# Random-feature projections of a pair's two heads: from one full-array product per slot to three products on each half of TensorE's rows

## The chip, the cores and the metric

The kernel runs on one core of one Trainium2 chip. What counts is the device time of one execution in microseconds (us), so lower is better. TensorE (PE in the profile) multiplies matrices: a weight load (PEld) puts the stationary operand in the array, and a matmul streams the moving operand past it into PSUM. VectorE (DVE), ScalarE (ACT) and GpSimd (POOL) do the elementwise work, SyncE (SP) issues the DMAs.

## What is computed

```python
B, H, S, D, M = 8, 8, 576, 64, 128           # batch, heads, tokens, head size, features
def phi(x):                                  # x already scaled by D ** -0.25
    h = einsum('bhsd,md->bhsm', x, omega) - sum(x * x, -1) / 2
    return exp(h - max(h, -1)) / sqrt(M)
q_p, k_p = phi(q_s), phi(k_s)
kv, z = k_p^T v, sum of k_p over tokens      # per head
attn = (q_p kv) / (q_p z + 1e-6)
x = attn as [4608 tokens, 512]
out = elu(x @ w_in) @ w_out                  # w_in 512 x 2048, w_out 2048 x 512, both float64
```

All in float32 precision. Attention is linear in the number of tokens; the two layers after it (the MLP) are most of the arithmetic.

## The kernel before

**Attention.** The 64 heads are taken as 32 pairs (two heads that lie side by side, `pair`). A pair's 1152 rows (2 x 576 tokens) make nine slots of 128 tokens: slot j < 8 belongs to head j % 2, and slot 8 holds the last 64 tokens of both heads. Each pair has a key side and a query side. `project` turns one side into the features `h` (128 tokens x 9 slots x 128 features); `kv` multiplies the key features with the values; `finish` spreads z over the partitions, divides the query features by their denominators, transposes them (`pt`) and multiplies them with kv (`pn`) into the MLP's input, split in a head `xh` and a tail `xl`.

**Two kinds of sides.** On a "native" side (`i < NNAT[nm]`: the first 7 key sides and 8 query sides) the projection is plain float32: the rows of x and their squares, 128 partitions deep, against `of` (omega over -SCALE/2). The profile counts two weight loads and two matmuls for each such float32 product. On the other 49 sides, x is split in a head `hi` (rounded to float32r) and a tail `lo` = x - hi, and omega in `oh` and `ol`. Before the change, hi and lo of one head lie above each other in the 128 rows (`t`, written by four copies and subtractions of 64 partitions), and one float32r matmul with 256 moving columns `[oh | ol]` (line 488) gives hi.oh + lo.oh in the left half and hi.ol + lo.ol in the right half of a PSUM bank. So there are nine such matmuls per side, two to a bank, five banks. ACT moves the right half and half the sum of squares to `p2` (line 497), DVE subtracts it from the left half and takes the largest value in the same operation (line 506), ACT negates it (line 410) and takes the exponential of `h` in SBUF (line 404).

**MLP.** Twelve blocks of 384 tokens and sixteen slices of 128 hidden features; the first three blocks go through in two halves of eight slices. One of the 192 steps is twelve matmuls of 384 columns (layer 1, three products of heads and tails for each of four chunks, lines 764 to 766, into `ph`), an ELU on ACT, DVE and POOL, and nine matmuls of 512 columns (layer 2, lines 798 to 800, into `acc`). Weights come as float64 and are converted by ACT, DVE and POOL during the first block.

**What sets the order.** Nothing is issued as the code reads. Every piece of work is a task (`op`) with an engine, an assumed time and a due time; `Plan.order` plays them through with these assumed times, giving each free engine the ready task with the earliest due time (some tasks may go to one of two engines), and the instructions are written in that order. Due times come from the constants at the head (`SEG`, `STEP`, `DUE_K`, `K2` and so on), the assumed time of a float32r matmul from `mm`. PSUM has eight banks: three `acc`, two `ph`, three `pa`; projections of later pairs, `pt` and `pn` share the three `pa`.

Of the kernel before, what the change touches and what calls it, by code (L numbers as in the profile page):

```python
# [14 lines left out]
ALU = mybir.AluOpType  # L15
# [25 lines left out]
NNAT = dict(k=7, q=8)  # L41
# [3 lines left out]
SEG = [8.62, 6.25, 4.29, 5.37, 3.5, 5.81]  # L45
STEP = 4.91
STEP_ATT = 6.59

LAG = 3.5


PAIR0 = 9.46
DUE_LOAD, DUE_K, DUE_KV, DUE_Q = 27.64, 24.71, 14.12, 18.02
LOAD2, K2, KV2, Q2 = 56.0, 46.17, 30.64, 29.89
TAIL = 11.71
TAIL2 = 4.06


CONV1 = 13.71
CONV_STEP = -0.51  # L60
CONV2 = 0.84
CONV3 = 70.47
# [5 lines left out]
DUE_Z = 12.0  # L68
# [195 lines left out]
def mm(n, m=1):  # L264

    return m * (n / 2.4 + 2.5)
# [15 lines left out]
def performer_elu_kernel(  # L282
# [31 lines left out]
    nc.vector.memset(of[D:P], -0.5 * SCALE)  # L314

# [22 lines left out]
    def omega(due):  # L338
        op("SP", 500, due + 0.005, lambda: nc.sync.dma_start(of[0:D], omT), (), ("of",), D * M * 4)
        t = Buf(sb, [P, M], F32, "junk", "omf", 2)  # L340
        due += 15
        for a in range(2):
            r = slice(a * D, a * D + D)
            op("SP", 500, due, lambda r=r: nc.sync.dma_start(t()[r], omT), (), ((t, a),), D * M * 4)
        op("DVE", dve(M), due + 3, lambda: nc.vector.tensor_copy(om[:, 0:M], t()), ((t, 0), (t, 1)), ("oh",))
# [22 lines left out]
    def bank(i, early, name):  # L368

        tag = early if i < NEARLY else "pa"  # L370
        return Buf(ps, [P, 512], F32, tag, name, dict(pa=3, ph=2).get(tag, 1))

# [21 lines left out]
    def project(i, nm, due):  # L394
# [6 lines left out]
        def exps(g, js, src, due, reads):  # L401
            def f():
                for j in js:
                    nc.scalar.activation(  # L404
                        h()[:, j, :], src(j), AF.Exp, bias=nb()[:, j:j + 1], scale=SCALE
                    )
            op("ACT", len(js) * act(M, native(i, nm), True), due, f, (*reads, (nb, g)), ((h, g),))

        def negate(g, js, due):
            op("ACT", act(4), due, lambda: nc.scalar.mul(nb()[:, js], mx()[:, js], -SCALE), ((mx, g),), ((nb, g),))  # L410

        if native(i, nm):
# [11 lines left out]
            for g in range(3):  # L424
                d = due + 2.2 * g
                p = bank(i, "acc%d" % g, f"pp{nm}_{i}_{g}")
                n = 4 if g < 2 else 1
                js = slice(4 * g, 4 * g + n)

                def mms(g=g, p=p):  # L430
                    for c in range(4 if g < 2 else 2):
                        t, a = 2 * g + c // 2, c % 2
                        if g < 2:
                            o = p()[:, c * M:(c + 1) * M]
                        else:
                            o = p()[a * D:a * D + D, 0:M]
                        nc.tensor.matmul(o, x()[:, a, t * P:min(t * P + P, S)], of, start=True, stop=True)

                def view(p=p):
                    return p().rearrange("p (j x) -> p j x", j=4)  # L440

                op("PE", 872 if g < 2 else 240, d, mms, [*((x, a, 2) for a in range(2)), "of"], (p,))
                op(
                    "DVE", 66 + n * 133, d + 1,
                    lambda js=js, n=n, view=view: nc.vector.tensor_reduce(mx()[:, js], view()[:, 0:n], AX.X, ALU.max),
                    (p,), ((mx, g),),
                )
                negate(g, js, d + 1.1)
                exps(g, range(js.start, js.stop), lambda j, g=g, view=view: view()[:, j - 4 * g], d + 1.5, (p,))
            return  # L450

        def t():
# [4 lines left out]
            lambda: nc.scalar.activation(t(), t(), AF.Square, scale=(SCALE * 0.5) ** 0.5), ((x, 3),), ((x, 3),),  # L457
# [3 lines left out]

        y = Buf(sb, [P, 2 * S], F32R, "t", f"t{nm}_{i}", 2)
        for a in range(2):
            r, o = slice(a * D, a * D + D), slice(D - a * D, P - a * D)
            cs = slice(a * S, a * S + S)
            parts = ((x, 0),)
            op(
                "ACT", act(S), due - 5 + a, lambda e, r=r, cs=cs: copy(e, y()[r, cs], x()[r, 0]), parts, ((y, a, "h"),),  # L470
                alt=other("y_hi", "DVE", dve(S, True)),
            )
            op(
                "POOL", pool(S), due - 4 + a,
                lambda e, r=r, o=o, cs=cs: tt(e, y()[o, cs], x()[r, 0], y()[r, cs].bitcast(F32), ALU.subtract),
                (*parts, (y, a, "h")), ((y, a, "l"),), alt=other("y_lo", "DVE", dve(S)),
            )
        for c in range(5):
            d = due + 1.1 * c
            p = Buf(ps, [P, 512], F32, "pa", f"pp{nm}_{i}_{c}", 3)  # L480
            p2 = Buf(sb, [P, 2, M], F32, "p2", f"p2{nm}_{i}_{c}", 2)
            n = 2 if c < 4 else 1
            g = 0 if c < 2 else 1

            def mms(c=c, p=p, n=n):
                for a in range(n):
                    o = a * (S + D) + c * P
                    nc.tensor.matmul(p()[:, a * 256:(a + 1) * 256], y()[:, o:o + P], om, start=True, stop=True)  # L488

            def view(p=p):  # L490
                return p().rearrange("p (a x) -> p a x", a=2)

            op("PE", mm(256, n), d, mms, [(y, a, z) for a in range(2) for z in "hl"] + ["oh", "om"], (p,))
            def rest(c=c, n=n, p2=p2, view=view):
                for a in range(n):
                    j = 2 * c + a
                    nc.scalar.activation(  # L497
                        p2()[:, a], view()[:, a, M:], AF.Identity, bias=sq()[:, j:j + 1], scale=-1.0
                    )

            op("ACT", n * act(M, True, True), d + 0.5, rest, (p, sq), (p2,))

            def ttr(c=c, n=n, p2=p2, view=view):
                for a in range(n):
                    j = 2 * c + a
                    nc.vector.tensor_tensor_reduce(  # L506
                        out=h()[:, j, :], in0=view()[:, a, 0:M], in1=p2()[:, a, :], scale=1.0, scalar=LOWEST,
                        op0=ALU.subtract, op1=ALU.max, accum_out=mx()[:, j:j + 1],
                    )

            op("DVE", n * 212, d + 1, ttr, (p, p2), ((h, g, c), (mx, g)))
            if c in (1, 4):
                js = range(0, 4) if c == 1 else range(4, NJ)
                negate(g, slice(js.start, js.stop), d + 1.1)
                exps(g, js, lambda j: h()[:, j, :], d + 1.5, [(h, g, e) for e in range(5)])

    def parts_of(i, nm):
        h = st[i]["h" + nm]
        return [(h, g) for g in range(3 if native(i, nm) else 2)]
# [38 lines left out]
    def finish(i, due):  # L558
# [15 lines left out]
        for g in range(3):  # L574
            d = due - 9 + g
            js = slice(4 * g, min(4 * g + 4, NJ))
            n = js.stop - js.start
            slots = [(j, j % 2, slice(0, P)) for j in range(4 * g, 4 * g + 4)]
            if g == 2:
                slots = [(8, a, slice(a * D, a * D + D)) for a in range(2)]  # L580
            hg = (h, g) if native(i, "q") else (h, min(g, 1))

            def dens(slots=slots):
                for j, a, r in slots:
                    junk = Buf(sb, [P, M], F32, "junk", f"junk_{i}_{j}_{a}", 2)
                    nc.vector.tensor_tensor_reduce(  # L586
                        out=junk()[r], in0=h()[r, j, :], in1=pz()[r, a * P:(a + 1) * P], scale=1.0, scalar=EPS,
                        op0=ALU.mult, op1=ALU.add, accum_out=den()[r, j:j + 1],
                    )

            def dg(js=js):
                return den()[:, js]

            op("DVE", len(slots) * 210, d, dens, (hg, pz), ((den, g),))
# [4 lines left out]
                    e, h()[:, js], h()[:, js], den()[:, js].unsqueeze(2).to_broadcast([P, n, M]), ALU.mult  # L599
# [5 lines left out]
            def turn(g=g, p=p, js=js):  # L605
                for e, j in enumerate(range(js.start, js.stop)):
                    nc.tensor.transpose(p()[:, e * P:(e + 1) * P], h()[:, j, :], ident)  # L607

            def src(g=g, p=p):
                if g == 2:  # L610
                    return p()[:, 0:P].rearrange("p (a x) -> p a x", a=2)
                return p().rearrange("p (t a x) -> p a t x", t=2, a=2)

            def dst(x, g=g):
                if g == 2:
                    return x[:, :, 512:S]
                return x[:, :, g * 256:(g + 1) * 256].rearrange("p a (t x) -> p a t x", t=2)
# [332 lines left out]
```

## Time and profile before

| | |
|---|---|
| device time, three runs | median 1089.97 us (1088.09 to 1090.83) |
| profiled execution, span from first to last instruction | 1090.7 us, the only time given for it |
| PE busy | 1060.6 us, 97% of the span, 5971 matmuls |
| PE weight loads busy | 936.8 us (86%) |
| ACT, DVE, POOL busy | 724.7 us (66%), 635.9 us (58%), 404.4 us (37%) |
| DMA | 176.90 MB, 162 GB/s |

In the rows of the timeline a matmul's own time includes its way through the array, so the times of two that follow each other overlap; what one costs is the distance from its start to the start of the next. A row with xN is N instructions in a row, merged. `128*128` is the number of active rows and columns of the array; `128*64` uses half of the columns, and two such matmuls can stand beside each other.

### The profile page before, as it was taken

The numbers are of one execution on the slowest core, as the hardware profiler recorded it, in microseconds if no ns is written. First come the engines' busy times: TensorE is split into PE (matmuls) and PEld (weight loads), VectorE is DVE, ScalarE is ACT, GpSimd is POOL, SyncE is SP. The second block draws the span as 40 slices with busy tenths as digits, with TensorE's granted clock in tenths as the row PEclk, the third lists the DMA queues.
The fourth block names the chain that finished last, engine by engine and source line by source line (L and its number), as shares of the span: only waits on it lengthen the run. The fifth ranks groups of instructions, "written<-read, shape, count | busy, mean of one in ns | idle before, by whom it ended". The sixth has DMA issues, their size and how long they took to land.

```text
span 1090.7 us, 19072 instructions
## 1 busy us (share of the span) xinstructions
PE 1060.6 (97%) x5971; PEld 936.8 (86%) x5971; DVE 635.9 (58%) x2403; ACT 724.7 (66%) x2027; POOL 404.4 (37%) x372
## 2 busy tenths in 40 slices
PE   7979888999999999999999999999999999999998
PEld 7867777889988888999888888899888888899987
DVE  6788988775776775225676666324566775322221
ACT  6878774546988986337888988326888888432222
POOL 3568746661223343222343233322233342222221
PEclk8889998999999999999999999999999999999999
DMA  7554656656663554434554645434444452343431
GB/s 213 171 181 161 208 188 240 218 186 205 207 205 130 169 170 150 165 118 157 176 155 153 193 139 170 162 119 150 162 155 167 157 164 79 117 164 119 161 121 63
DMA packets 53235, 176.90 MB, mean 162 GB/s; under 512 B 6032, under 2 KB 6224, under 8 KB 53136
## 3 DMA queue, kind: packets, MB, share of 16 engines
q1 hardware_dynamic: 53136, 175.69, 48.4%
q8 instruction: 48, 0.79, 0.3%
q14 instruction: 51, 0.42, 0.1%
HBM read 155.48 MB, written 20.19 MB: 161 GB/s over the span
## 4 chain that ended last, share of the span: by engine, by line
PE 79%; DVE 9%; ACT 6%; issue 3%; DMA 1%; POOL 1%; SPq 0%; DVEq 0%; POOLq 0%; ACTq 0%
PE ph L764 11%; PE acc L798 10%; PE acc L800 10%; PE ph L766 10%; PE acc L799 10%; PE ph L765 10%; PE pkv L535 4%; PE ppq L488 3%; PE pn L634 3%; PE pt L607 2%; PE ppk L488 2%; ACT hk L404 1%; DVE u_w L697 1%; DVE u_w L704 1%; DVE u_w L709 1%
## 5 line engine op out<-in xcount | busy, mean ns | idle before, releaser
L336 POOL TENSOR_TENSOR g<-e,g 128x384 fp32r<-128x384 f32 x182 | 189.2, 1040 | 547.7 <-DVE g L333 405.9
L764 PE MATMUL ph<-xh,w1c 128*128 128x384 f32 x768 | 267.5, 348 | 6.7 <-DVE e L777 6.2
L766 PE MATMUL ph<-xh,w1c 128*128 128x384 f32 x768 | 259.8, 338 | 0.0
L765 PE MATMUL ph<-xl,w1c 128*128 128x384 f32 x768 | 259.7, 338 | 0.0
L777 DVE SCALAR_TENSOR_TENSOR e<-e,ph 128x384 f32<-128x384 f32 x192 | 105.9, 552 | 237.2 <-ACT e L774 232.8
L798 PE MATMUL acc<-w2h,g 128*128 128x512 f32 x576 | 231.4, 402 | 0.0
L773 ACT ACTIVATE e<-ph 128x384 f32<-128x384 f32 x192 | 93.6, 488 | 206.4 <-PE ph L766 198.4
L800 PE MATMUL acc<-w2h,g 128*128 128x512 f32 x576 | 227.7, 395 | 0.0
L799 PE MATMUL acc<-w2l,g 128*128 128x512 f32 x576 | 227.4, 395 | 0.0
L764 PEld LDWEIGHTS ph<-xh,w1c 128*128 128x128 f32 x768 | 145.6, 190 | 20.1 <-DVE e L777 8.5
L765 PEld LDWEIGHTS ph<-xl,w1c 128*128 128x128 f32 x768 | 145.8, 190 | 7.2
L766 PEld LDWEIGHTS ph<-xh,w1c 128*128 128x128 f32 x768 | 145.4, 189 | 0.3 <-POOL w1c L336 0.3
L800 PEld LDWEIGHTS acc<-w2h,g 128*128 128x128 f32 x576 | 108.5, 188 | 25.5
L798 PEld LDWEIGHTS acc<-w2h,g 128*128 128x128 f32 x576 | 108.7, 189 | 15.1 <-issue 2.3
L799 PEld LDWEIGHTS acc<-w2l,g 128*128 128x128 f32 x576 | 108.8, 189 | 12.2
L336 POOL TENSOR_TENSOR hq<-hq,den 128x512 f32<-128x512 f32 (+1 forms) x96 | 90.4, 961 | 36.1 <-DVE den L595 24.6
L774 ACT ACTIVATE e<-e 128x384 f32<-128x384 f32 x192 | 100.7, 525 | 3.1
L333 DVE CAST g<-e 128x384 fp32r<-128x384 f32 x166 | 72.8, 439 | 23.5 <-PE acc L800 18.8
L586 DVE CUSTOM_DVE_ANT_0 junk<-hq,pz 128x128 f32<-128x128 f32 (+1 forms) x320 | 74.1, 279 | 16.9 <-PE pz L570 16.1
L506 DVE CUSTOM_DVE_ANT_0 hq<-ppq,p2q 128x128 f32<-128x128 f32 x216 | 54.3, 287 | 41.8 <-ACT p2q L497 40.2
L506 DVE CUSTOM_DVE_ANT_0 hk<-ppk,p2k 128x128 f32<-128x128 f32 x225 | 56.5, 286 | 36.1 <-ACT p2k L497 34.3
L497 ACT ACTIVATE p2q<-ppq,sqq 128x128 f32<-128x128 f32 x216 | 67.8, 367 | 12.5 <-PE ppq L488 10.8
(82 smaller groups left out, 1620.3 us busy)
## 6 DMA issues: line engine op xcount, KB each, us to landing
w1c<-w1s SPq DMA_DIRECT2D x176, 512.0 KB, 3.3
raw_w<-in_w_dram SPq DMA_DIRECT2D x32, 512.0 KB, 3.6
xk<-in_kx_dram SPq DMA_DIRECT2D x25, 576.0 KB, 3.9
xq<-in_qx_dram SPq DMA_DIRECT2D x24, 576.0 KB, 4.6
v<-in_v_dram SPq DMA_DIRECT2D x32, 325.0 KB, 3.4
out_dram<-o SPq DMA_DIRECT2D x36, 256.0 KB, 2.9
w1s<-w1c SPq DMA_DIRECT2D x16, 512.0 KB, 3.2
xq<-in_q_dram SPq DMA_DIRECT2D x8, 288.0 KB, 4.0
```

What stands on the lines that cost most here:

```text
L336: (nc.vector if e == "DVE" else nc.gpsimd).tensor_tensor(*args)
L506: nc.vector.tensor_tensor_reduce(out=h()[:, j, :], in0=view()[:, a, 0:M], in1=p2()[:, a, :], scale=1.0, scalar=LOWEST, op0=ALU.subtract, o ...
L586: nc.vector.tensor_tensor_reduce(out=junk()[r], in0=h()[r, j, :], in1=pz()[r, a * P:(a + 1) * P], scale=1.0, scalar=EPS, op0=ALU.mult, op1 ...
L764: nc.tensor.matmul(ph(), wh, xh[:, c, o:o + TB], start=(c == 0), stop=False)
L765: nc.tensor.matmul(ph(), wh, xl[:, c, o:o + TB], start=False, stop=False)
L766: nc.tensor.matmul(ph(), wl, xh[:, c, o:o + TB], start=False, stop=(c == NC - 1))
L773: op("ACT", act(TB, True), due, lambda: nc.scalar.activation(e(), ph(), AF.Relu, scale=-1.0), (p,), (e,))
L774: op("ACT", act(TB), due + 0.2, lambda: nc.scalar.activation(e(), e(), AF.Exp, scale=-1.0), (e,), (e,))
L777: lambda: nc.vector.scalar_tensor_tensor(e(), e(), -1.0, ph(), ALU.add, ALU.max), (p, e), (e,),
L798: nc.tensor.matmul(a(), g()[:, 0, ts], w2h[:, f], start=(f == f0), stop=False)
L799: nc.tensor.matmul(a(), g()[:, 0, ts], w2l[:, f], start=False, stop=False)
L800: nc.tensor.matmul(a(), g()[:, 1, ts], w2h[:, f], start=False, stop=(f == f1 - 1))
```

## The change

It replaces the projection of all sides that are not native and makes twelve sides native (5 key sides, 7 query sides) where there were fifteen.

- `t` now holds hi and lo in two planes of 128 rows: head 0 in rows 0 to 63, head 1 in rows 64 to 127. One copy and one subtraction of 128 partitions make it.
- Slots 0 to 7: for each of four chunks, three products hi.oh, lo.oh and hi.ol of 64 rows and 128 columns are summed in PSUM for either head (line 507), head 0 into one bank and head 1 into another, the two heads taking turns: 24 matmuls in one task.
- Slot 8: two float32 matmuls of 128 rows into 64 columns each (line 515), straight from x, against `oz`, which is omega in one half of its rows and zero in the other.
- `p2` is gone. DVE takes the largest values of four slots at once from PSUM (line 428), two small operations make the bias from it and the sum of squares (lines 482 and 483), and ACT takes the exponential from PSUM (line 419). Slots of one head now form a group, so groups take every second slot.
- The assumed time of a float32r matmul goes from n / 2.4 + 2.5 to n / 2.25 + 2.5 ns, and most due times are other ones.

```diff
-NNAT = dict(k=7, q=8)
+NNAT = dict(k=5, q=7)
-SEG = [8.62, 6.25, 4.29, 5.37, 3.5, 5.81]
-STEP = 4.91
-STEP_ATT = 6.59
+SEG = [10.92, 6.51, 5.27, 5.54, 3.5, 5.81]
+STEP = 5.77
+STEP_ATT = 5.1
...
+    oz = const.tile([P, 2, M], F32, name="oz")
+    nc.vector.memset(oz, 0.0)
...
-        y = Buf(sb, [P, 2 * S], F32R, "t", f"t{nm}_{i}", 2)
-        for a in range(2):
-            r, o = slice(a * D, a * D + D), slice(D - a * D, P - a * D)
...
-        for c in range(5):
...
-            def mms(c=c, p=p, n=n):
-                for a in range(n):
-                    o = a * (S + D) + c * P
-                    nc.tensor.matmul(p()[:, a * 256:(a + 1) * 256], y()[:, o:o + P], om, start=True, stop=True)
...
+        def bias(g, js, due):
+            def f():
+                r = cols(js)
+                nc.vector.scalar_tensor_tensor(mx()[:, r], mx()[:, r], SCALE, sq()[:, r], ALU.mult, ALU.subtract)
+                nc.vector.scalar_tensor_tensor(nb()[:, r], mx()[:, r], -1.0, sq()[:, r], ALU.mult, ALU.subtract)
...
+        y = Buf(sb, [P, 2, S], F32R, "t", f"t{nm}_{i}", 2)
...
+        banks = [bank(i, "acc%d" % g, f"pp{nm}_{i}_{g}") for g in range(3)]
+        terms = ((0, 0), (1, 0), (0, M))
+
+        def mms():
+            for c in range(4):
+                for n, (z, m) in enumerate(terms):
+                    for a in range(2):
+                        r, o = slice(a * D, a * D + D), a * D + c * P
+                        nc.tensor.matmul(
+                            banks[a]()[:, c * M:(c + 1) * M], y()[r, z, o:o + P], om[r, m:m + M],
+                            start=(n == 0), stop=(n == 2),
+                        )
+
+        def last():
+            for a in range(2):
+                o = (1 - a) * (S - D)
+                nc.tensor.matmul(
+                    banks[2]()[a * D:a * D + D, 0:M], x()[:, 0, o:o + D], oz[:, a], start=True, stop=True
+                )
+
+        op("PE", mm(M, 12), due, mms, ((y, "h"), (y, "l"), "oh", "om"), banks[0:2])
+        op("PE", 230, due + 2, last, ((x, 0), ("oz", 0), ("oz", 1)), banks[2:3])
```

On PE, here is the key side of pair 26, in the middle of the MLP's ninth block, before. `ppk` is the side's PSUM bank, `tk` its heads and tails, `ph` and `acc` are the MLP's.

```order
L765 MATMUL ph_132_9251<-xl_82,w1c_132_9031 128x384
L766 MATMUL ph_132_9251<-xh_81,w1c_132_9031 128x384
L488 MATMUL ppk_26_0_9280<-om_73,tk_26_9042 128x256 x2
L798 MATMUL acc_8_0_0_9108<-w2h_77,g_130_9152 128x512
L799 MATMUL acc_8_0_0_9108<-w2l_78,g_130_9152 128x512
L800 MATMUL acc_8_0_0_9108<-w2h_77,g_130_9152 128x512
L488 MATMUL ppk_26_1_9293<-om_73,tk_26_9042 128x256 x2
```

And the same side after; between the second and the third row stand the other 22 matmuls of line 507, `ppk_26_0` and `ppk_26_1` by turns.

```order
L507 MATMUL ppk_26_0_9215<-om_73,tk_26_9016 128x128
L507 MATMUL ppk_26_1_9217<-om_73,tk_26_9016 128x128
...
L813 MATMUL acc_8_0_0_9241<-w2h_79,g_128_8987 128x512
L814 MATMUL acc_8_0_0_9241<-w2l_80,g_128_8987 128x512
L815 MATMUL acc_8_0_0_9241<-w2h_79,g_128_8987 128x512
L779 MATMUL ph_132_9201<-xh_83,w1c_132_8996 128x384
L780 MATMUL ph_132_9201<-xl_84,w1c_132_8996 128x384
L781 MATMUL ph_132_9201<-xh_83,w1c_132_8996 128x384
L515 MATMUL ppk_26_2_9251<-oz_75,xk_26_8949 64x128 x2
L813 MATMUL acc_8_0_1_9259<-w2h_79,g_128_8987 128x512
```

Five short pieces spread between the MLP's matmuls have become one block of 24 and one of two, each with full-array matmuls on both sides. In the whole program, the places where PE goes over to products of half the array (64 rows or 64 columns) and back were 46; now they are 144.

On ACT, the same side before, from its first operation after the projection to its last:

```order
L497 ACTIVATE p2k_26_0_9300<-ppk_26_0_9280,sqk_26_8839 128x128 x2
L404 ACTIVATE hq_25_9182<-hq_25_9182,nbq_25_9233 128x128 x5
L774 ACTIVATE e_132_9290<-e_132_9290 128x384
L497 ACTIVATE p2k_26_1_9331<-ppk_26_1_9293,sqk_26_8839 128x128 x2
L497 ACTIVATE p2k_26_2_9338<-ppk_26_2_9317,sqk_26_8839 128x128 x2
L410 ACTIVATE nbk_26_9348<-mxk_26_9314 128x4
L497 ACTIVATE p2k_26_3_9350<-ppk_26_3_9325,sqk_26_8839 128x128 x2
L404 ACTIVATE hk_26_9313<-hk_26_9313,nbk_26_9348 128x128 x4
L497 ACTIVATE p2k_26_4_9375<-ppk_26_4_9353,sqk_26_8839 128x128
```

and after:

```order
L788 ACTIVATE e_132_9263<-ph_132_9201 128x384
L419 ACTIVATE hk_26_9268<-ppk_26_0_9215,nbk_26_9255 128x128 x4
L789 ACTIVATE e_132_9263<-e_132_9263 128x384
L419 ACTIVATE hk_26_9268<-ppk_26_1_9217,nbk_26_9255 128x128 x4
L419 ACTIVATE hk_26_9268<-ppk_26_2_9251,nbk_26_9255 128x128
L336 CAST tk_27_9339<-xk_27_9273 128x576
```

The nine operations of line 497 and the two of line 410 are gone, and the copy that makes `tk` of the next pair is one of 128 partitions where there were two of 64.

More of the change, by code (lines that the diff above doesn't have):

```diff
@@ L38 @@
 F64_MAX = float.fromhex("0x1.dffffep-96")
-NNAT = dict(k=7, q=8)
+NNAT = dict(k=5, q=7)
 MLP0 = 58
-SEG = [8.62, 6.25, 4.29, 5.37, 3.5, 5.81]
-STEP = 4.91
-STEP_ATT = 6.59
[L49 to L59, printed above, removed]
+SEG = [10.92, 6.51, 5.27, 5.54, 3.5, 5.81]
+STEP = 5.77
+STEP_ATT = 5.1
+LAG = 3.75
+PAIR0 = 8.73
+DUE_LOAD, DUE_K, DUE_KV, DUE_Q = 30.22, 22.83, 16.48, 18.02
+LOAD2, K2, KV2, Q2 = 56.0, 37.39, 30.64, 29.89
+TAIL = 14.11
+TAIL2 = 4.77
+CONV1 = 13.86
 CONV_STEP = -0.51
-CONV2 = 0.84
-CONV3 = 70.47
+CONV2 = 1.42
+CONV3 = 55.14
+PACE = 2.25
 SPLIT = (0, 8, 16)
 NHALF = 3
-DUE_Z = 12.0
+DUE_Z = 11.71
 NEARLY = 4
@@ L264, in mm @@
 def mm(n, m=1):
-    return m * (n / 2.4 + 2.5)
+    return m * (n / PACE + 2.5)
 def act(n, psum=False, ptr=False):
@@ L371, in bank, with slots, cols @@
         return Buf(ps, [P, 512], F32, tag, name, dict(pa=3, ph=2).get(tag, 1))
+    def slots(i, nm, g):
+        if g == 2:
+            return range(8, 9)
+        return range(4 * g, 4 * g + 4) if native(i, nm) else range(g, 8, 2)
+    def cols(js):
+        return slice(js.start, js.stop, js.step)
     def load_pair(i, due):
@@ L399, in project, with exps, largest @@
         mx, nb = small("mx" + nm, NJ, f"mx{nm}_{i}"), small("nb" + nm, NJ, f"nb{nm}_{i}")
-        def exps(g, js, src, due, reads):
+        def exps(g, js, p, due):
             def f():
-                for j in js:
+                for e, j in enumerate(js):
                     nc.scalar.activation(
-                        h()[:, j, :], src(j), AF.Exp, bias=nb()[:, j:j + 1], scale=SCALE
+                        h()[:, j, :], p()[:, e * M:(e + 1) * M], AF.Exp, bias=nb()[:, j:j + 1], scale=SCALE
                     )
-            op("ACT", len(js) * act(M, native(i, nm), True), due, f, (*reads, (nb, g)), ((h, g),))
-        def negate(g, js, due):
-            op("ACT", act(4), due, lambda: nc.scalar.mul(nb()[:, js], mx()[:, js], -SCALE), ((mx, g),), ((nb, g),))
+            op("ACT", len(js) * act(M, True, True), due, f, (p, (nb, g)), ((h, g),))
+        def largest(g, js, p, due):
+            n = len(js)
+            op(
+                "DVE", 66 + n * 133, due,
+                lambda: nc.vector.tensor_reduce(
+                    mx()[:, cols(js)], p()[:, 0:n * M].rearrange("p (j x) -> p j x", x=M), AX.X, ALU.max
+                ),
+                (p,), ((mx, g),),
+            )
         if native(i, nm):
@@ L437, in mms @@
                         nc.tensor.matmul(o, x()[:, a, t * P:min(t * P + P, S)], of, start=True, stop=True)
-                def view(p=p):
-                    return p().rearrange("p (j x) -> p j x", j=4)
                 op("PE", 872 if g < 2 else 240, d, mms, [*((x, a, 2) for a in range(2)), "of"], (p,))
+                largest(g, js, p, d + 1)
                 op(
-                    "DVE", 66 + n * 133, d + 1,
-                    lambda js=js, n=n, view=view: nc.vector.tensor_reduce(mx()[:, js], view()[:, 0:n], AX.X, ALU.max),
-                    (p,), ((mx, g),),
-                )
-                negate(g, js, d + 1.1)
-                exps(g, range(js.start, js.stop), lambda j, g=g, view=view: view()[:, j - 4 * g], d + 1.5, (p,))
+                    "ACT", act(4), d + 1.1,
+                    lambda js=js: nc.scalar.mul(nb()[:, cols(js)], mx()[:, cols(js)], -SCALE), ((mx, g),), ((nb, g),),
+                )
+                exps(g, js, p, d + 1.5)
             return
@@ L460, in project @@
         op("DVE", dve(S), due - 3, lambda: nc.vector.tensor_reduce(sq(), t(), AX.X, ALU.add), ((x, 3),), (sq,))
-        y = Buf(sb, [P, 2 * S], F32R, "t", f"t{nm}_{i}", 2)
-        for a in range(2):
-            r, o = slice(a * D, a * D + D), slice(D - a * D, P - a * D)
[L467 to L477, printed above, removed]
@@ L478, in project @@
-        for c in range(5):
[L479 to L483, printed above, removed]
-            def mms(c=c, p=p, n=n):
-                for a in range(n):
-                    o = a * (S + D) + c * P
[L488 to L515, printed above, removed]
@@ new lines, in bias @@
+        def bias(g, js, due):
[3 more added lines that the diff above has]
+                nc.vector.scalar_tensor_tensor(nb()[:, r], mx()[:, r], -1.0, sq()[:, r], ALU.mult, ALU.subtract)
+            op("DVE", 2 * dve(4), due, f, ((mx, g), sq), ((mx, g), (nb, g)))
+        y = Buf(sb, [P, 2, S], F32R, "t", f"t{nm}_{i}", 2)
+        op(
+            "ACT", act(S), due - 5, lambda e: copy(e, y()[:, 0], x()[:, 0]), ((x, 0),), ((y, "h"),),
+            alt=other("y_hi", "DVE", dve(S, True)),
+        )
@@ new lines, in project @@
+        op(
+            "POOL", pool(S), due - 4,
+            lambda e: tt(e, y()[:, 1], x()[:, 0], y()[:, 0].bitcast(F32), ALU.subtract), ((x, 0), (y, "h")),
+            ((y, "l"),), alt=other("y_lo", "DVE", dve(S)),
+        )
+        banks = [bank(i, "acc%d" % g, f"pp{nm}_{i}_{g}") for g in range(3)]
[8 more added lines that the diff above has]
+                            start=(n == 0), stop=(n == 2),
+                        )
@@ new lines, in last @@
+        def last():
[3 more added lines that the diff above has]
+                    banks[2]()[a * D:a * D + D, 0:M], x()[:, 0, o:o + D], oz[:, a], start=True, stop=True
+                )
+        op("PE", mm(M, 12), due, mms, ((y, "h"), (y, "l"), "oh", "om"), banks[0:2])
+        op("PE", 230, due + 2, last, ((x, 0), ("oz", 0), ("oz", 1)), banks[2:3])
+        for g, p in enumerate(banks):
+            d = due + 1.2 + 1.8 * g
+            js = slots(i, nm, g)
+            largest(g, js, p, d)
+            bias(g, js, d + 0.1)
+            exps(g, js, p, d + 0.5)
@@ L517, in parts_of @@
     def parts_of(i, nm):
         h = st[i]["h" + nm]
-        return [(h, g) for g in range(3 if native(i, nm) else 2)]
+        return [(h, g) for g in range(3)]
     def kv(i, due):
@@ L575, in finish, with dens @@
             d = due - 9 + g
-            js = slice(4 * g, min(4 * g + 4, NJ))
-            n = js.stop - js.start
-            slots = [(j, j % 2, slice(0, P)) for j in range(4 * g, 4 * g + 4)]
+            js = slots(i, "q", g)
+            n = len(js)
+            jobs = [(j, j % 2, slice(0, P)) for j in js]
             if g == 2:
[L580 to L584, printed above, removed]
+                jobs = [(8, a, slice(a * D, a * D + D)) for a in range(2)]
+            hg = (h, g)
+            def dens(jobs=jobs):
+                for j, a, r in jobs:
                     junk = Buf(sb, [P, M], F32, "junk", f"junk_{i}_{j}_{a}", 2)
@@ L605, in turn @@
             def turn(g=g, p=p, js=js):
-                for e, j in enumerate(range(js.start, js.stop)):
+                for e, j in enumerate(js):
                     nc.tensor.transpose(p()[:, e * P:(e + 1) * P], h()[:, j, :], ident)
@@ L611, in src @@
                     return p()[:, 0:P].rearrange("p (a x) -> p a x", a=2)
+                if not native(i, "q"):
+                    return p()
                 return p().rearrange("p (t a x) -> p a t x", t=2, a=2)
@@ L616, in dst @@
                     return x[:, :, 512:S]
+                if not native(i, "q"):
+                    return x[:, g, 0:512]
                 return x[:, :, g * 256:(g + 1) * 256].rearrange("p a (t x) -> p a t x", t=2)
```

12 lines of the change are left out of this document (6 added, 6 removed).

## Prediction

> **What bounds the kernel now.** First the page's busy times and its chain that ended last.
>
> ```profile
> span 1090.7 us, 19072 instructions
> PE 1060.6 (97%) x5971; PEld 936.8 (86%) x5971; DVE 635.9 (58%) x2403; ACT 724.7 (66%) x2027; POOL 404.4 (37%) x372
> PE 79%; DVE 9%; ACT 6%; issue 3%; DMA 1%; POOL 1%; SPq 0%; DVEq 0%; POOLq 0%; ACTq 0%
> ```
>
> PE is busy for 97% and makes up most of the chain; ACT, which loses the most work, is at 66%. An average can hide stages, so next the windows.
>
> ```profile
> core 0: us, PE busy (x) PEld busy (x) DVE busy (x) ACT busy (x) POOL busy (x), PEclk, DMA share, GB/s
> 0.00:200.00 200.00, 175.61 (x1032) 150.25 (x1033) 161.95 (x445) 146.86 (x409) 121.01 (x102) 0.93 0.59 194
> 200.00:950.00 750.00, 747.95 (x4257) 663.62 (x4256) 444.70 (x1895) 540.41 (x1545) 250.45 (x239) 1.00 0.48 160
> 950.00:1091.00 141.00, 137.02 (x686) 122.95 (x685) 29.25 (x64) 37.44 (x73) 32.95 (x33) 1.00 0.36 125
> ```
>
> There are two stages. From 200 to 950 us PE idles 2 us in 750 at full clock: nobody keeps it waiting, and only its own work counts. Before 200 us it idles 24 us and runs at 0.93 of its clock (another 14), so at most 38 us can be had there from other engines. Where do the changed projections lie?
>
> ```profile
> L488 PE MATMUL ppk<-om,tk x225: 276/282/385, 117.5 to 913.8; 128*128 128x256 f32 x113
> L488 PE MATMUL ppq<-om,tq x216: 273/282/391, 262.4 to 929.8; 128*128 128x256 f32 x108
> ```
>
> All but a few are in the second stage. So the question is only whether PE's own work grows or shrinks, and busy times don't tell, since they overlap; starts do.
>
> **What the old projection costs PE.** The timeline of PE:
>
> ```profile
> 301.14 0.40 PE L799 MATMUL acc<-w2l,g 128*128 128x512 f32 x1
> 301.38 0.40 PE L800 MATMUL acc<-w2h,g 128*128 128x512 f32 x1
> 301.61 0.64 PE L488 MATMUL ppq<-om,tq 128*128 128x256 f32 x4
> 302.09 0.39 PE L798 MATMUL acc<-w2h,g 128*128 128x512 f32 x1
> ```
>
> From 301.61 to 302.09 four matmuls of 256 columns take 0.48 us, 0.12 each, and they slip between the MLP's (0.23 or 0.24 from start to start) with nothing added. A side has nine: 1.08 us; 49 sides: 52.9 us.
>
> **What the new block of 24 costs.** No matmul before uses 64 rows, so its price is bounded from the nearest rows. In 128 columns stream 0.06 us (half of 0.12). But each matmul brings its own weights. Weight loads, where nothing hides them:
>
> ```profile
> 40.69 0.63 PEld L437 LDWEIGHTS ppk<-of,xk 128*128 128x128 f32 x5 [0.17 <-issue]
> 311.89 0.19 PEld L798 LDWEIGHTS acc<-w2h,g 128*128 128x128 f32 x1 [0.49 <-DVE tk L336]
> 312.00 0.19 PEld L799 LDWEIGHTS acc<-w2l,g 128*128 128x128 f32 x1
> 313.65 1.00 PE L535 MATMUL pkv<-v,hk 128*128 128x65 f32 x8
> 314.46 0.48 PE L488 MATMUL ppq<-om,tq 128*128 128x256 f32 x2
> ```
>
> Lines 798 and 799 are float32r: the second load starts 0.11 us after the first. The native line 437: (0.63 - 0.19) / 4 = 0.11. And kv's matmuls of 65 columns, half as long as ours, still come only every (314.46 - 313.65) / 8 = 0.10. So a 128-column load takes PE 0.11 us, and a matmul shorter than that doesn't hide it. For the new block: at best loads don't bind and both halves run together, 0.06 a pair; at worst all loads share one path, 0.22 a pair; between, the halves load side by side, 0.11 a pair. I take 0.11, because halves side by side is what the trace shows for column halves, the nearest thing:
>
> ```profile
> 310.33 0.33 PE L765 MATMUL ph<-xl,w1c 128*128 128x384 f32 x1
> 310.51 0.33 PE L766 MATMUL ph<-xh,w1c 128*128 128x384 f32 x1
> 310.77 1.19 PE L634 MATMUL pn<-qh,kvf 128*64 128x256 f32 x8
> 311.89 0.50 PE L798 MATMUL acc<-w2h,g 128*128 128x512 f32 x1
> 312.22 0.40 PE L799 MATMUL acc<-w2l,g 128*128 128x512 f32 x1
> 39.79 0.60 PE L607 MATMUL pt<-ident,hq 128*128 128x128 f32 x4
> 40.33 0.44 PE L437 MATMUL ppq<-of,xq 128*64 128x128 f32 x4
> 40.70 0.94 PE L437 MATMUL ppk<-of,xk 128*128 128x128 f32 x6
> ```
>
> Four native matmuls on column halves (40.33) leave in 0.37 us, though 0.11 each one after another would be 0.44, and that 0.37 has a switch in it (below). Twelve pairs: 1.32 us a side.
>
> The Trainium skill ("TensorE: Matmul & The Clock Gate", LDWEIGHTS) says that a load's time goes by its columns and not its rows; the 0.11 agrees as far as columns go, and no run here shows 64 rows. Its section "Measured speedup vs the span model" would give a pack of two halves the time of one matmul and 4 ns more, about 0.064 a pair as an estimate: by that the sum below would be some 29 us lower.
>
> **What going over to half the array costs.** The same fence. A 384-column matmul is followed after 0.18 us (310.33 to 310.51), so `pn` could start at 310.69; it starts at 310.77, 0.08 to 0.09 late. After it line 798 takes 0.33 to the next (311.89 to 312.22), not 0.23: its successor's weights couldn't be loaded ahead, 0.10 more. And the block at 40.33 lasts 0.37 for two pairs of 0.11, 0.15 more. An excursion thus costs 0.09 + 0.15 + 0.10 = 0.34 us beside its matmuls. The order has 144 where it had 46: 98 x 0.34 = 33.3 us. For 64 rows no row shows it; if those blocks switch for nothing, 52 x 0.34 = 17.7 us of it fall away.
>
> **Slot 8 and the sides that change kind.** Line 515 is the same pair of float32 products as the native line 437's block: 0.22 us beside its excursion. A native side has 16 full matmuls of 0.11 and this block, 1.98 us; three such sides go: -5.9 us.
>
> **Sum for PE.** 52 x (1.32 + 0.22) = 80.1; minus 52.9; minus 5.9; plus 33.3: **+54.6 us**.
>
> **The other engines.**
>
> ```profile
> L404 ACT ACTIVATE hk<-hk,nbk 128x128 f32<-128x128 f32 x225 | 71.4, 397 | 0.5
> L497 ACT ACTIVATE p2k<-ppk,sqk 128x128 f32<-128x128 f32 x225 | 68.3, 364 | 8.1 <-PE ppk L488 7.2 <-DVE mxk L506 0.7
> L506 DVE CUSTOM_DVE_ANT_0 hk<-ppk,p2k 128x128 f32<-128x128 f32 x225 | 56.5, 286 | 36.1 <-ACT p2k L497 34.3
> L331 ACT CAST tk<-xk 64x576 fp32r<-64x576 f32 x50 | 33.6, 672 | 1.2 <-PE ppk L488 0.5
> L506 DVE DVE_READ_ACCUMULATOR2_ANT mxk<- 128x1 f32 x225 | 18.5, 82 | 0.0
> L404 ACT ACTIVATE hk<-ppk,nbk 128x128 f32<-128x128 f32 x63 | 18.3, 376 | 0.1
> L445 DVE TENSOR_REDUCE mxk<-ppk 128x4 f32<-128x512 f32 x14 | 9.6, 685 | 2.3 <-PE ppk L437 2.2
> L410 ACT ACTIVATE nbk<-mxk 128x4 f32<-128x4 f32 x39 | 8.2, 211 | 3.8 <-DVE mxk L506 1.7 <-DVE mxk L445 1.3
> ```
>
> ACT loses per side nine operations of 364 ns, two of 211 and one copy of 672, some 4.4 us; its exponentials cost about the same (397 from SBUF, 376 from PSUM). DVE loses nine of 286 + 82 (3.3 us) and gains two reductions of 685, a short one and six tiny operations, each between the 82 and the 211 of the small ones here: about a microsecond saved. Over 49 sides ACT is relieved by 216 us, and I count it at nothing: from 200 us on, PE idles 2 us, so there is nobody to hand it to. New is a wait in the other direction: the block needs two of the three `pa` banks at once, and a bank comes free after a reduction, the bias and four exponentials, 0.7 + 0.4 + 1.5 = 2.6 us. Behind it PE's whole queue would stand; what covers it is the MLP between two sides, 750 / 49 = 15 us each. Uncovered at every side it would be 52 x 2.6 = 135 us, which two engines with more spare time than before speak against. The two loads of `oz` and three sides with 576 instead of 288 KB go over DMA engines with 0.48 in use: nothing.
>
> **Early stage.** At most 38 us to be had; later blocks could as well start later by some 10. ACT and DVE lose little there (few sides of the new kind), and the order on PE of the first two batches is nearly the old one; I take -8.
>
> So 1090.7 + 54.6 - 8 = 1137.3; the median of the runs lies 0.7 under the span: **1137 us**.
>
> **Rivals.**
> (a) One load path: the halves' loads go one after another, as full-array loads do at 312.00; 0.22 a pair, 52 x 12 x 0.11 = 69 us more: 1206. For it: no row with two loads of 64 rows. Against it: column halves share better.
> (b) Loads are hidden in a pair, each half loading while the other streams: 0.06 a pair, 31 us less: 1106. For it: only full loads are seen to bind. This is the rule of the span model above. Against it: kv's 0.10 for 65 columns.
> (c) Faster. A block of 64-row products is cheap altogether, 0.06 a pair and no switch: 54.6 - 31.2 - 17.7 = +5.7 us on PE. Then the stage before 200 us decides: when the new due times win more than 6 of its 38 us, the kernel is faster; with half of them, 19, 1077. For it: the idle time there is real, and fewer steps lie between a projection and its exponentials. Against it: 0.11 per load, and 0.09 + 0.15 + 0.10 on every switch that is seen.
> That the change doesn't do what it says is excluded by the order, which shows 24 and 2 matmuls per side.
>
> **Chances.** Forecast 56% (1115 to 1150: without the switch of row blocks 1119, with a stage before 200 us that loses a little 1150), (a) 16%, (b) 10%, (c) 18%. Differences within 0.3% (3 us) can't be told from none. Faster: (c) but for 3%, and 2% from the others: 17%. The same: 5%. Slower: 78%. The range goes from near (c) to (a), 1080 to 1208.
>
> **What would show it.** In the new timeline: starts of line 507 in pairs, the pairs 0.11 apart (0.06 for b, c; 0.22 or single starts 0.11 apart for a). The first of line 507 about 0.09 behind its turn, and a matmul after line 507 or 515 that takes 0.10 more than usual. PE busy 98 or 99% after 200 us with ACT below 60%; ACT busy some 200 us less and the span longer all the same. I am wrong if PE idles after 200 us (then it is the banks), or if the MLP's first block ends much sooner than before.

## The result, and the profile after

The changed kernel is slower: 1151.65 us in the median (1149.5 to 1152.27) against 1089.60 us for the kernel before (four runs of each), a ratio of 1.0567 with a 95% interval of 1.0546 to 1.0587. 62 us were lost where 47 were forecast; the profiled execution's span went from 1090.7 to 1150.5 us. The page of the kernel after, its busy times and the chain that ended last:

```profile
span 1150.5 us, 19651 instructions
PE 1114.9 (97%) x6926; PEld 959.8 (83%) x6926; DVE 612.3 (53%) x1922; ACT 567.7 (49%) x1455; POOL 386.8 (34%) x363
PE 83%; DVE 10%; issue 2%; DMA 2%; POOL 1%; ACT 1%; SPq 0%; POOLq 0%; DVEq 0%; ACTq 0%
```

ACT does 157 us less, DVE 24 us less, PE 54 us more, and the span follows PE. The windows, with the same two stages (columns as before):

```profile
0.00:200.00 200.00, 173.18 (x1071) 147.53 (x1072) 160.08 (x430) 130.11 (x355) 120.70 (x102) 0.92 0.59 189
200.00:1010.00 810.00, 805.07 (x5175) 688.93 (x5174) 423.48 (x1430) 401.24 (x1030) 232.70 (x228) 1.00 0.46 151
1010.00:1151.00 141.00, 136.64 (x684) 123.33 (x682) 28.72 (x63) 36.31 (x71) 33.44 (x33) 1.00 0.37 124
```

After 200 us PE still idles only 5 us in 810, with ACT at half load: the second stage is longer because PE has more to do. The first 200 us look as before (PE 173.2 us busy instead of 175.6). How one key side looks in the timeline of PE, the block of 24 and later slot 8:

```profile
514.29 0.39 PE L815 MATMUL acc<-w2h,g 128*128 128x512 f32 x1
514.61 1.56 PE L507 MATMUL ppk<-om,tk 64*128 64x128 f32 x24
516.10 0.50 PE L813 MATMUL acc<-w2h,g 128*128 128x512 f32 x1
516.44 0.40 PE L814 MATMUL acc<-w2l,g 128*128 128x512 f32 x1
...
518.98 0.34 PE L781 MATMUL ph<-xh,w1c 128*128 128x384 f32 x1
519.25 0.44 PE L515 MATMUL ppk<-oz,xk 128*64 128x128 f32 x4
519.62 0.44 PE L779 MATMUL ph<-xh,w1c 128*128 128x384 f32 x1
519.90 0.34 PE L780 MATMUL ph<-xl,w1c 128*128 128x384 f32 x1
```

The block's loads in the timeline of PEld, and those of slot 8:

```profile
514.61 1.42 PEld L507 LDWEIGHTS ppk<-om,tk 64*128 64x128 f32 x24 [0.36 <-issue]
519.25 0.20 PEld L515 LDWEIGHTS ppk<-oz,xk 128*64 128x64 f32 x4 [0.25 <-issue]
```

The block starts 0.32 us after a matmul that otherwise gives way after 0.23: 0.09 late. From its start to the next start it takes 1.49 us. The matmul behind it takes 0.34 (516.10 to 516.44) and not 0.23: 0.11. Its 24 loads come in twelve pairs; a load itself lasts 0.19, so the last pair starts (1.42 - 0.19) = 1.23 us after the first, 1.23 / 11 = 0.112 a pair. Twelve pairs are 1.34 of the 1.49, so 0.15 is lost inside the block. Slot 8: 0.27 instead of 0.18 ahead of it, 0.37, and 0.28 instead of 0.17 behind it. A side thus costs PE 1.49 + 0.20 + 0.37 + 0.20 = 2.26 us where it cost 1.08.

Where the time went shows best by progress. Layer 1's first line runs four times a step; its 129th matmul (33rd step) starts at 249.8 us before and at 254.6 after, its 705th (177th step) at 1013.8 and 1073.7. Up to the 33rd step 4.8 us were lost, from there to the 177th, when all attention is done, 55.2 us. Of the 52 changed sides 4 lie before the 33rd step and 48 between the two; of the 49 before the change, 2 and 47.

The 4.8 us arise in one place. At the 21st step (195 us) the changed kernel is 0.8 us ahead, at the 25th it is 4.2 us behind. Between them stand this wait and, in the windows, six microseconds at half the clock:

```profile
210.81 0.69 PE L779 MATMUL ph<-xh,w1c 128*128 128x384 f32 x1 [2.86 <-DVE e L792]
210.00:216.00 6.00, 5.19 (x15) 4.71 (x16) 5.93 (x9) 2.29 (x4) 3.73 (x4) 0.50 0.40 115
```

PE stands 2.86 us for DVE's part of an ELU (`e`); on DVE, conversions of the weights and the ELU of an earlier step stand ahead of it. After the wait the clock is granted at 0.50. This is one execution, and the longest of its four, so part of the 4.8 us may belong to it alone.

### The profile page after: what moved, and what is told of

Same layout as the page of the kernel before. It is cut to its first block, busy times and chain, and to the rows that moved or that the text cites. A ratio compares the mean times of both kernels' runs of the same rounds, so it can differ in the third digit from the quotient of the medians.

```text
span 1150.5 us, 19651 instructions
## 1 busy us (share of the span) xinstructions
PE 1114.9 (97%) x6926; PEld 959.8 (83%) x6926; DVE 612.3 (53%) x1922; ACT 567.7 (49%) x1455; POOL 386.8 (34%) x363
## 4 chain that ended last, share of the span: by engine, by line
PE 83%; DVE 10%; issue 2%; DMA 2%; POOL 1%; ACT 1%; SPq 0%; POOLq 0%; DVEq 0%; ACTq 0%
PE ph L779 12%; PE acc L813 11%; PE ph L781 10%; PE ph L780 10%; PE acc L814 10%; PE acc L815 10%; PE pkv L546 4%; PE ppq L507 3%; PE ppk L507 3%; PE pn L649 3%; PE pt L618 2%; DVE u_w L719 1%; DVE u_w L712 1%; DMA xq<-in_q_dram 1%; DVE u_w L724 1%
## 5 line engine op out<-in xcount | busy, mean ns | idle before, releaser
L779 PE MATMUL ph<-xh,w1c 128*128 128x384 f32 x768 | 275.4, 359 | 8.1 <-DVE e L792 8.1
L781 PE MATMUL ph<-xh,w1c 128*128 128x384 f32 x768 | 260.3, 339 | 0.0
L780 PEld LDWEIGHTS ph<-xl,w1c 128*128 128x128 f32 x768 | 146.0, 190 | 10.5
L419 ACT ACTIVATE hk<-ppk,nbk 128x128 f32<-128x128 f32 x288 | 83.3, 382 | 50.6 <-DVE nbk L483 25.6
L419 ACT ACTIVATE hq<-ppq,nbq 128x128 f32<-128x128 f32 x288 | 83.5, 382 | 45.4 <-DVE mxq L482 38.6
L341 POOL TENSOR_TENSOR hq<-hq,den 128x512 f32<-128x512 f32 (+1 forms) x96 | 85.2, 906 | 58.1 <-DVE den L606 53.4
L338 DVE CAST g<-e 128x384 fp32r<-128x384 f32 x141 | 56.8, 403 | 86.1 <-PE acc L815 84.0
L428 DVE TENSOR_REDUCE mxk<-ppk 128x4 f32<-128x512 f32 (+1 forms) x96 | 51.0, 553 | 35.0 <-PE ppk L507 31.0
```

The lines of the kernel that those rows point to most:

```text
L341: (nc.vector if e == "DVE" else nc.gpsimd).tensor_tensor(*args)
L419: nc.scalar.activation(h()[:, j, :], p()[:, e * M:(e + 1) * M], AF.Exp, bias=nb()[:, j:j + 1], scale=SCALE)
L779: nc.tensor.matmul(ph(), wh, xh[:, c, o:o + TB], start=(c == 0), stop=False)
L780: nc.tensor.matmul(ph(), wh, xl[:, c, o:o + TB], start=False, stop=False)
L781: nc.tensor.matmul(ph(), wl, xh[:, c, o:o + TB], start=False, stop=(c == NC - 1))
```

## The experiments

Two theories stood against each other. Mine: the loss is PE's own work, a load of 0.11 us for each pair and 0.34 us for each going over to half the array. The other: something else lost it, the new due times, or waits on banks and engines. Each run has its own comparison with the kernel before, so ratios are compared; spans are of one profiled execution each. That of the change itself is 1.0567.

**Old constants.** The new projection with the constants of before (15 native sides, old due times, 2.4 for 2.25):

```diff
-NNAT = dict(k=5, q=7)
+NNAT = dict(k=7, q=8)
-SEG = [10.92, 6.51, 5.27, 5.54, 3.5, 5.81]
+SEG = [8.62, 6.25, 4.29, 5.37, 3.5, 5.81]
...
-PACE = 2.25
+PACE = 2.4
```

> The new projection with the old constants (due times, assumed rate, fifteen native sides). Theory: PE's work is that of the change within 1 us, so 1152 us, 1146 to 1158. Rival (due times made the loss): 1120 or less. Rival (due times win and the projection costs even more): 1165 or more.

Measured: 1147.90 us, ratio 1.0499 (1.0461 to 1.0538). The loss is there without any new due time, so it belongs to the projection; the new constants win nothing with it, and rather cost some 0.7% (the two intervals just miss each other, and the runs were not side by side).

**New constants on the old projection.**

```diff
-SEG = [8.62, 6.25, 4.29, 5.37, 3.5, 5.81]
+SEG = [10.92, 6.51, 5.27, 5.54, 3.5, 5.81]
...
-NNAT = dict(k=7, q=8)
+NNAT = dict(k=5, q=7)
-    return m * (n / 2.4 + 2.5)
+    return m * (n / PACE + 2.5)
```

> The old projection (line 488, nine matmuls a side) with the new constants: due times, assumed matmul rate and twelve native sides. Theory (PE's own work decides): three native sides of 1.98 us of matmuls become three of 1.08 and five excursions to half the array fall away, -4.4 us on PE, so 1085 us if the due times are neutral, 1080 to 1092. Rival (the new due times cost a good part of the 62 us): 1100 us or more. Rival (they win what was hoped of the first 200 us): 1075 or less.

Measured: 1133.80 us, ratio 1.0359 (1.0323 to 1.0396). My 1085 was far off: with the old projection the new constants cost 40 us. The 33rd step starts 27 us later than before, the 177th 42. The first 200 us, and a stretch of the chain of waits inside them:

```profile
0.00:200.00 200.00, 157.36 (x892) 131.06 (x893) 165.46 (x497) 146.27 (x420) 109.63 (x92) 0.86 0.55 178
```

```profile
162.25 0.34 DVE u_w L707
163.01 1.28 DVE u_w L712
164.29 0.67 DVE sqk L463
164.96 0.98 DVE u_w L700
...
168.01 0.60 DVE u_w L712
169.06 1.30 DVE tk L339
170.70 1.43 DVE tk L339
```

PE is busy 18 us less than before, its clock is granted at 0.86, and for these microseconds the chain runs through DVE alone: conversion of the weights (`u_w`) and, between it, a sum of squares and the tails (`tk`, two of 1.3 and 1.4 us) of a key side that PE takes up only at 291 us. So the early stage is sensitive after all, and two runs took the constants apart.

**Fewer native sides alone**, in the kernel before:

```diff
-NNAT = dict(k=7, q=8)
+NNAT = dict(k=5, q=7)
```

> The kernel before with one constant pair changed, 5 and 7 native sides for 7 and 8: three sides of the first two batches go over to the old projection with p2. It tells which half of the constants cost the old projection 40 us in the run with all of them. Theory A (the old projection's extra DVE and ACT work in the first 200 us did it, three sides of some 4 us more on either engine where DVE was the chain): 1105 to 1125. Theory B (the due times did it): 1085 to 1097.

Measured: 1098.38 us, ratio 1.0072 (1.0046 to 1.0098), just above the range of theory B. **Due times and assumed rate**, the kernel before with all new constants but 7 and 8 native sides:

> The kernel before with all new constants but the native sides, which stay 7 and 8. Theory A: 1090 to 1105. Theory B (due times made for another projection): 1115 to 1135.

Measured: 1121.01 us, ratio 1.0302 (1.0268 to 1.0337). Theory B holds for the larger part: due times and assumed rate cost the old projection 3.0% (the rate by itself 1.05%, see the run below), the native sides 0.7%, together about the 3.6% of both. With the native sides of before PE stood longer not only at first (the first figure with an (x...) behind it is PE's busy time; in the kernel before it is 175.61 and 199.10 us for these two stretches):

```profile
0.00:200.00 200.00, 168.67 (x1011) 145.57 (x1012) 159.22 (x440) 140.52 (x395) 113.65 (x96) 0.93 0.57 187
200.00:400.00 200.00, 191.28 (x1061) 167.15 (x1060) 141.96 (x511) 143.54 (x403) 79.34 (x70) 0.99 0.56 186
```

PE is busy 7 and 8 us less in these two stretches; the 33rd step is 9 us late and the 177th 26. So less than half of the delay arises in the early stage. In the changed kernel the same constants cost little (0.7% against the old ones; its 33rd step is 4.8 us late, not 27). It may be that the relief of ACT and DVE carries constants which the old projection can't bear, and so buys no time; no run shows that it is this relief.

**Heads not by turns.** The same 24 matmuls, twelve of head 0 and then twelve of head 1:

```diff
-            for c in range(4):
-                for n, (z, m) in enumerate(terms):
-                    for a in range(2):
+            for a in range(2):
+                for c in range(4):
+                    for n, (z, m) in enumerate(terms):
```

> The 24 matmuls of a block issued as twelve of head 0 and then twelve of head 1 instead of by turns. Theory (a weight load of 0.11 us per matmul, two at a time only because the heads take turns on the two halves): 24 x 0.11 = 2.64 us a block instead of 1.32, +69 us over 52 sides, 1205 to 1222 us. Rival (TensorE runs the halves beside each other in whatever order they come): within 5 us of 1152.

Measured: 1205.08 us, ratio 1.1014 (1.0956 to 1.1072); span 1200.4, 50 us more than the change. One block in PE's timeline:

```profile
579.61 2.51 PE L507 MATMUL ppk<-om,tk 64*128 64x128 f32 x24
582.04 0.50 PE L813 MATMUL acc<-w2h,g 128*128 128x512 f32 x1
```

2.43 us instead of 1.49: 0.94 x 52 = 49 us, about all of the difference. The loads of this block, line 507 alone (the second figure with an (x...) counts the weight loads):

```profile
579.60:580.55 0.95, 0.94 (x8) 0.94 (x9) 1.00 1.04 403
```

Nine loads begin here, at 0.11 us each and with none beside them: that is the price of one half's loads, the same as that of a pair by turns. The tenth comes 0.07 us after the ninth, out of their step: head 1 begins there, beside the last three of head 0; so the block takes 2.43 us and not the 2.64 that I had put in. The halves do work side by side, but for most of a block only when the heads take turns.

**Twice the columns.** Every matmul of the block streams the 256 columns of omega's head and tail:

```diff
-                            banks[a]()[:, c * M:(c + 1) * M], y()[r, z, o:o + P], om[r, m:m + M],
+                            banks[a]()[:, (c % 2) * 2 * M:(c % 2 + 1) * 2 * M], y()[r, z, o:o + P], om[r],
```

> Each of the 24 matmuls streams 256 columns instead of 128 under the same weights (the whole of omega's head and tail), and chunks 2 and 3 overwrite 0 and 1, so the result is another. Theory (the load of 0.11 us sets the pace of a pair, 128 columns of 0.06 are hidden under it): a pair goes from 0.11 to 0.12, +6 us in all, 1152 to 1162. Rival (the stream sets the pace, 128 columns of float32r take 0.11 on half the rows): twice the columns, 0.22 a pair, +69 us, 1205 to 1225.

Measured: 1158.21 us, ratio 1.0586 (1.0538 to 1.0633), in the expected range; the span is 6.6 us longer than that of the change.

```profile
562.60 1.70 PE L507 MATMUL ppk<-om,tk 64*128 64x256 f32 x24
564.23 0.50 PE L813 MATMUL acc<-w2h,g 128*128 128x512 f32 x1
```

Twice the multiplications take 1.63 us instead of 1.49, 7 us over 52 sides. The loads set the pace of the block; about half of its time the array had room. That settles the forecast's open choice, and against the rival with hidden loads.

**Full array.** Both heads in one matmul of 256 columns, with omega in a block diagonal: the same three products, twelve matmuls a side, no going over for these (slot 8 still goes over). The preparation of omega and the grouping of the slots change with it.

```diff
-                    for a in range(2):
-                        r, o = slice(a * D, a * D + D), a * D + c * P
-                        nc.tensor.matmul(
-                            banks[a]()[:, c * M:(c + 1) * M], y()[r, z, o:o + P], om[r, m:m + M],
+                    o = (c % 2) * 2 * M
+                    nc.tensor.matmul(
+                        banks[c // 2]()[:, o:o + 2 * M], y()[:, z, c * P:(c + 1) * P],
+                        om[:, m].rearrange("p a x -> p (a x)"), start=(n == 0), stop=(n == 2),
```

> The products of both heads in one full-array matmul of 256 columns: the weights are 128 rows of both heads, the moving operand is omega's head (or tail) in a block diagonal, so twelve matmuls a side at 0.12 us and no going over to half the array. Theory: 1.44 us instead of 1.32 + 0.36, -0.24 x 52 = -12.5 us against the change, 1139 us, 1134 to 1144. Rival (going over to half the rows is cheap, the loss sits elsewhere): 12 x 0.12 instead of 1.32, +6 us, 1158.

Measured: 1138.72 us, ratio 1.0428 (1.0390 to 1.0467), as expected.

```profile
559.50 0.34 PE L775 MATMUL ph<-xh,w1c 128*128 128x384 f32 x1
559.68 1.61 PE L505 MATMUL ppk<-om,tk 128*128 128x256 f32 x12
561.12 0.39 PE L807 MATMUL acc<-w2h,g 128*128 128x512 f32 x1
561.35 0.39 PE L808 MATMUL acc<-w2l,g 128*128 128x512 f32 x1
```

1.44 us, no delay ahead (0.18) and none behind (0.23). Filling half the array with zeros is cheaper here than using its halves apart: 1.44 instead of 1.49 + 0.20.

**And slot 8 on the full array.** Three float32r products with zeros in the weights, x padded by 64 columns:

```diff
-            for a in range(2):
-                o = S - D
-                nc.tensor.matmul(
-                    banks[2]()[a * D:a * D + D, 0:M], x()[:, 0, o:o + D], oz[:, a], start=True, stop=True
-                )
+            for n, (z, m) in enumerate(terms):
+                nc.tensor.matmul(
+                    banks[2]()[:, 0:M], y()[:, z, 512:W], os[:, m], start=(n == 0), stop=(n == 2)
+                )
```

> The same, and slot 8 too on the full array: three float32r matmuls of 128 columns (0.33 us) with zeros in the weights, instead of a pair of float32 products on column halves (0.22 + 0.34). Theory: another -0.23 x 52 = -12 us, 1127 us, 1121 to 1133; still above the kernel before, since a side then costs 1.77 us of PE and not 1.08. Rival (PE's work isn't all of the loss, waits on banks or engines are): 1140 or more.

Measured: 1134.38 us, ratio 1.0380 (1.0349 to 1.0412). That is just above the expected 1121 to 1133 and below the rival's 1140. The span went down by 10.5 us where 12 were expected (1141.5 to 1131.0), but the first of these two executions was the longest of its four and the second the shortest; the medians went down by 4, with intervals that overlap.

```profile
557.88 0.34 PE L778 MATMUL ph<-xh,w1c 128*128 128x384 f32 x1
558.06 0.45 PE L516 MATMUL ppk<-os,tk 128*128 128x128 f32 x3
558.34 0.45 PE L810 MATMUL acc<-w2h,g 128*128 128x512 f32 x1
558.63 0.40 PE L811 MATMUL acc<-w2l,g 128*128 128x512 f32 x1
```

0.28 us, and 0.06 behind it, since a load of 0.11 isn't hidden under 128 columns: 0.34 instead of 0.57. Sides still cost 1.44 + 0.34 = 1.78 us against 1.08, and the kernel stays 3.8% slower than before. From the 33rd to the 177th step it took 795 us, the full array alone 805, the change 819, the kernel before 764. The two steps back win 14 and 10 us there. One side more lies before the 33rd step in them, 47 between the two: 47 x (1.69 - 1.44) and that side's 2.26 make 14, 47 x (0.57 - 0.34) make 11, and of the 31 that are left 47 x (1.78 - 1.08) make 33. The 33rd step itself is later in both (260 us, the change 255), which the forecasts of these two runs left out.

**Blocks cut in two**, the second half due 2.5 us later:

```diff
-        op("PE", mm(M, 12), due, mms, ((y, "h"), (y, "l"), "oh", "om"), banks[0:2])
+        for k in range(2):
+            op(
+                "PE", mm(M, 6), due + 2.5 * k, lambda k=k: mms(range(2 * k, 2 * k + 2)),
```

> Each block of 24 cut in two tasks of twelve, the second due 2.5 us later, with the MLP's matmuls between; the order has 188 excursions where the change has 144, the products are the same. Theory (an excursion costs 0.34 to 0.36 us): +15 to +16 us, 1164 to 1171. Rival (only the first matmul after a block is late, 0.10): +4 us, 1156.

Measured: 1163.78 us, ratio 1.0654 (1.0622 to 1.0687), just under the expected range; the span is 12.1 us over the change's, by the ratios it is 9.5. For 44 more excursions that is 0.28 each or less, below my 0.34 to 0.36. The rows tell why:

```profile
579.42 0.44 PE L515 MATMUL ppq<-oz,xq 128*64 128x128 f32 x4
579.79 0.89 PE L507 MATMUL ppq<-om,tq 64*128 64x128 f32 x12
580.61 0.45 PE L784 MATMUL ph<-xh,w1c 128*128 128x384 f32 x1
580.90 0.34 PE L785 MATMUL ph<-xl,w1c 128*128 128x384 f32 x1
```

A half block takes 0.82, two take 0.15 more than one whole of 1.49: every cut pays that. The 0.09 and 0.11 around a block are paid only towards full-array matmuls, and here the half block follows straight on slot 8. Of the 188 places 28 stand directly beside another of the half array, in the change 2 of the 144. So PE leaves the full array 18 times more and not 44: 44 x 0.15 + 18 x 0.20 = 10.2 us. The prices hold; my count was wrong.

**More work for ACT.** It copies every slot of the changed sides once more:

```diff
+            op("ACT", len(js) * act(M, False, True), d + 0.6, more, ((h, g),), (spare,))
```

> ACT copies each of the nine slots of the 52 sides once more into a spare buffer after the exponentials, 52 x 9 x 0.37 us = 173 us of work, about what the change took off it. Theory (ACT's work is hidden, so what the change saved there was worth nothing): within 4 us of 1152. Rival (the lighter ACT did win something that covers part of the loss): 1160 or more.

Measured: 1154.04 us, ratio 1.0567 (1.0528 to 1.0606), that of the change. The page's busy times:

```profile
PE 1114.0 (97%) x6926; PEld 958.9 (83%) x6926; DVE 618.3 (54%) x1951; ACT 644.3 (56%) x1899; POOL 378.9 (33%) x358
```

ACT is busy 77 us more (copies that follow each other overlap, so not the 173 of my estimate), and nothing happens to the time. So about half of what the change took off ACT is shown to be worth nothing there.

**A better version?** Two runs on the kernel before looked for time in its first 200 us. The assumed matmul rate as the trace has it:

```diff
-    return m * (n / 2.4 + 2.5)
+    return m * (n / 2.25 + 2.5)
```

> The kernel before with the assumed time of a float32r matmul taken from the trace (n / 2.25 instead of n / 2.4), nothing else. Only the order can change, and from 200 us on PE has no idle time to win: 1085 to 1097. If it is below 1085, an order from truer times wins in the first 200 us, which would be a version better than both.

Measured: 1100.86 us, ratio 1.0105 (1.0082 to 1.0129): a little slower, and outside the expected range. Its 33rd step is 0.2 us late and its 177th 11: the loss falls in the second stage, where PE now idles 8 us in the 800 from 200 to 1000 us and before 2. That nobody keeps PE waiting there holds for the order of before, not for every order. And one more native side, so that all of the first two batches are:

```diff
-NNAT = dict(k=7, q=8)
+NNAT = dict(k=8, q=8)
```

> The kernel before with 8 and 8 native sides: the last side of the first two batches that went through p2 becomes native. PE: +1.98 + 0.34 - 1.08 = +1.2 us; DVE and ACT are relieved by some 4 us each in the first 200 us. Theory (PE's sum decides): 1088 to 1095. Rival (DVE and ACT set the pace of the first 200 us): 1080 to 1087, better than both kernels.

Measured: 1091.53 us, ratio 0.9999 (0.9979 to 1.0019): the same. Nothing tried beats the kernel before.

## Why the prediction was right, point by point

The direction and the mechanism came out: PE's own work, by the price of a pair of loads and of going over. The size was 15 us short, 1151.65 us where 1137 was forecast, and just above the 1115 to 1150 named for this case.

- **What bounds it.** Right. After 200 us the time is PE's own work: ACT lost 157 us and got 77 back in a run without any effect. The relief itself was forecast too large (216 us): operations of one kind overlap, and the 225 of line 497 that the forecast took at 364 ns had kept ACT busy for 68.3 us, 0.30 each; and ACT now makes 25 more casts of `g` (26.2 us instead of 13.4).
- **The pair of loads.** Forecast 0.11 us, between 0.06 and 0.22; 0.112 in the trace. Doubling the columns shows that it is the load and not the stream, and taking away the turns that two loads go side by side only when they belong to different halves.
- **Excursions.** Forecast 0.34 us (0.09, 0.15 and 0.10), with doubt whether 64-row blocks pay them. They do: 0.09 ahead and 0.11 behind, and 0.15 inside. That the 0.15 fits is in part luck: it was read off four matmuls on column halves as what 0.37 leaves over two pairs of loads at 0.11, but loads of 64 columns come faster there (in slot 8, with the same 0.37, all four are through in 0.20 and one lasts 0.13 to 0.14, so the pairs come 0.06 apart). On row halves the 0.15 is shown by itself, by 1.49 less twelve pairs and by the cut.
- **Slot 8.** Forecast 0.22 + 0.34 = 0.56; measured 0.57.
- **The sum for PE.** Forecast +54.6 us; from the 33rd to the 177th step the kernel lost 55.2. By the measured prices it is 52 x 2.26 - 52.9 - 3 x 2.32 = 57.7 (a native side at the forecast's 1.98 + 0.34), and 48 x 2.26 - 47 x 1.08 = 57.7 between these two steps, so nothing before the 33rd.
- **The early stage.** This is the step that failed. I took -8 us out of at most 38, on the ground that few sides change there; at the 33rd step the kernel was 4.8 us late. Those 12.8 us are nearly the whole distance between the forecast span (1137.3) and the measured one (1150.5). The ground was wrong: the stage is sensitive to the constants (the same ones cost the old projection 27 us there), but the new ones won nothing; with the old constants the new projection was 3.3 us late. What shows in place of the gain is one wait of 2.86 us for DVE and the half clock behind it. With the old constants the 3.3 us are there from the 13th step on, so that is another wait; which one stays open, and a few microseconds are also what executions of one kernel differ by.
- **Rivals.** (a) would show loads one after another: they come in pairs. (b) needs a pair at 0.06, (c) also blocks without a switch: both are excluded by the 0.112 and by the run with doubled columns, (c) also by the 0.09 and 0.11 around a block.

## What to carry to other kernels

A short matmul costs what its weight load costs (here 0.11 us for 128 columns): with 128 columns of weights for each, 24 products of 128 columns on half arrays need more time than nine of 256 on the full one, though they multiply less. Before splitting the array, count the loads, add a fixed price for going over and back (here 0.20 us around a block, 0.35 with what is lost inside), and compare with padding by zeros, which here was cheaper. And relief for engines that nobody waits for is no gain, however large: look first whether the engine that bounds the kernel idles in the stage where it falls.

## What had not been expected

- One number in the planner that was made truer (2.25 instead of 2.4 columns per ns, as the trace shows) made the kernel before 1.05% slower. It looks as if due times are fitted to the planner's errors, which no run shows; in any case they couldn't be carried over from one set of costs, or one projection, to another here (3.0% for the old projection with the new due times and rate).
- Of one half's loads one comes every 0.11 us, of both halves by turns a pair every 0.112: two halves load at twice the rate of one.
- A block that stands directly beside another one of the half array pays nothing towards it: the 0.09 and 0.11 are the price of the way between half and full array.
